# Five buffers for the values on their way out, a later fetch of the queries for the row maxima, and a later first subtraction of LayerNorm, in a gated attention and MLP block on one core

## The chip, the cores and the metric

The kernel runs on 1 core of one Trainium2 chip, as one launch. The metric is device microseconds of that launch; smaller is better. Times of whole runs are medians over a few runs; a profile is one further execution, taken with the hardware profiler. TensorE is PE in the rows (its weight loads are PEld), VectorE is DVE, ScalarE is ACT, GpSimd is POOL, SyncE is SP.

## The reference

One token block of 2048 rows and 448 features goes through two branches and a gate. Branch A is attention with 16 heads of 28 features, branch B a LayerNorm with a two-layer MLP of 1792 hidden features; a sigmoid of one dot product per row weighs them.

```python
def _A_ref(x, wqkv, wo):
    B, S, D = x.shape                      # 1, 2048, 448
    H = 16
    Dh = D // H
    qkv = (lambda x, *d: x.transpose(*d))((x @ wqkv).reshape(B, S, 3, H, Dh), 2, 0, 3, 1, 4)
    q, k, v = qkv[0], qkv[1], qkv[2]
    scores = jnp.einsum("bhqd,bhkd->bhqk", q, k) * (Dh ** -0.5)
    p = _softmax(scores, axis=-1)
    o = jnp.einsum("bhqk,bhkd->bhqd", p, v)
    return (lambda x, *d: x.transpose(*d))(o, 0, 2, 1, 3).reshape(B, S, D) @ wo

def _B_ref(x, w1, b1, w2, b2):
    y = _layernorm(x, axis=-1)
    h = _gelu(jnp.einsum("bsd,df->bsf", y, w1) + b1)
    return jnp.einsum("bsf,fd->bsd", h, w2) + b2

x = A_x
g = _sigmoid((x * gate_w).sum(-1, keepdims=True))
return g * _A_ref(x, A_wqkv, A_wo) + (1 - g) * _B_ref(x, B_w1, B_b1, B_w2, B_b2)
```

All arrays are float32. The kernel keeps that precision by splitting an operand into a rounded high part and a low rest and by adding three products (high by high, high by low, low by high).

## The kernel before

The program has two long parts, and both are ordered by hand: what PE does next is written out by Python code at build time.

**The strips** (class `Strips`, L404 to L538, up to about 455 us of the profile). PE is used as four strips of 32 rows. A tile of 128x512 (or 128x448) results lies in one PSUM bank; each strip adds its quarter of the contraction to it in a *visit* of 10 to 42 matmuls of 32 rows. Two strips don't visit a tile at the same time, and it is done when all four have. There are four kinds of tiles: `QK` (queries and keys, 28 of them), `Val` (the values with the gate's dot product as one more column, 16), `Up` (first MLP layer, 14 for each of four chunks of 512 tokens) and `Down` (second layer, 4 for each chunk). Six PSUM banks are for tiles, two (6 and 7) for row maxima.

**Row maxima.** The softmax needs a maximum for each query row before its exponentials are formed. It takes 1024 matmuls (L212: 28 rows of queries `qd` by 512 keys of `kd`), each followed by a `reduce_max` on DVE (L214). They are slipped between the visits whenever a planned bank and planned DVE time are free (`rowmax`, L497); what is left over at the end of the strips is slipped into the attention turns. They run in 16 problems `n` (4 groups of heads by 4 chunks of queries), problem `n` in buffer `qd[n % 2]`. When strip `j` has done its 16 matmuls of problem `n`, its quarter of the buffer is fetched anew for problem `n + 2` (`load_q`, L196, on SP's queue); after the last problem of a group its keys are fetched too (`load_k`, L180).

**The planner's clock.** The class simulates time: each matmul has a cost, each engine a time at which it comes free, and work of other engines is put on a list by `st.at(time, function)` and emitted when the planned time gets there. Only the order in which the instructions are emitted remains in the program; at run time each engine goes through its own list in order and waits on semaphores. A planned time that moves therefore moves instructions on every engine, and what PE does in the gaps changes with it.

**Handoffs.** When one strip ends its visit, the next strip may take the same bank only after it. This is signalled through SP: an increment of a semaphore, which waits for the last matmul of the visit, stands in SP's list, and the first matmul of the next visit waits for it. SP has the same list for its DMA issues, so an issue that waits, or that takes long, holds up the handoffs behind it.

```python
    sig = nc.sync.sem_inc(hand, 1)                                   # end of a visit, on SP (L529)
    tc.add_manual_dep(sig.ins, mm.ins.name, handoff, reason="handoff")
    ...
    if m == 0 and x.sig:                                             # start of the next one, on PE (L487)
        nc.tensor.wait_ge(hand, x.sig)
```

**Values on their way out.** When a `Val` tile is done, ACT copies it from PSUM to one of the buffers `vt` (L324) and a gate column to `zall` (L325), and then issues the store `vs<-vt` (L328) on its own queue. Tile `i` uses buffer `i % 3`. A copy waits until the store that used this buffer before has landed.

**LayerNorm.** For each chunk `c`, `want_ln` fetches the rows of mean and reciprocal deviation, spread over all partitions (`lnr`, L160, on POOL's queue), and four slices of x (`raw`, L571 on POOL's queue or, late, L569 on SP's). Each slice is then subtracted (L683 on DVE for chunks 0 and 1, L679 on POOL for 2 and 3), multiplied (L688 on POOL) and split into `yh` (L704, ACT) and `yl` (L705, POOL), which the `Up` tiles need. The same four slots `raw` also carry the weights w2 before that (w2's low parts are formed at L153 on POOL and DVE).

**The turns** (from about 455 us). Attention goes in turns of 5 or 6 units; a unit is 128 keys by 512 queries of one head, three score matmuls (L1152). After each half turn ACT forms exponentials of three or two banks at once (L1156), and PE multiplies them by the values (L1164). While row maxima are owed, a turn may have 5 units with three row-maximum matmuls, or 6 units with two; the planner takes as few turns of 5 as the owed number allows:

```python
size = min(left, 5 if owed and owed > 2 * ((left - 116) // 6) else 6)
```

Of the kernel before, what the change touches and what calls it, by code (L numbers as in the profile page):

```python
# [7 lines left out]
F32 = mybir.dt.float32  # L8
# [7 lines left out]
P = 128  # L16
S = 2048
D = 448
H = 16
# [16 lines left out]
def kernel(ctx: ExitStack, tc: tile.TileContext, xt, wqk, wv, wo, xk, w1, b1, w2, b2,  # L36
# [37 lines left out]
    bk = banks.tile([P, 8, CH], F32, name="bk")  # L74
# [3 lines left out]
    px = p0.enter_context(tc.tile_pool(name="px", bufs=1))  # L78
# [42 lines left out]
    mr = px.tile([P, 2, NT], F32, name="mr")  # L121
    mrt = px.tile([P, 2 * NT], F32, name="mrt")
    std = px.tile([P, NT], F32, name="std")
    vt = [px.tile([P, H, 32], F32, name=f"vt{i}") for i in range(3)]

    bxr = [px.tile([P, 2, D], F32, name=f"bxr{i}") for i in range(2)]

# [29 lines left out]
    def ln_rows_load(c):  # L157
        cs = slice(c * CH, (c + 1) * CH)
        lnr[c] = my.tile([P, 2, CH], F32, name="lnr")
        nc.gpsimd.dma_start(lnr[c], lns.rearrange("(n t) i -> n (t i)", n=2)[:, cs].partition_broadcast(P))  # L160

    class RowMax:
# [64 lines left out]
        def close(self, n):  # L227
            mf, mt = self.mf[n % 2], self.mt[n % 2]
            nc.vector.reduce_max(mf[:, 0:16], self.mx[n % 2].rearrange("p j i k -> p (j i) k"), axis=AX)
            nc.vector.transpose(mt, mf)  # L230
# [6 lines left out]
    rowmax = RowMax()  # L237
# [63 lines left out]
    class Val(Piece):  # L301
# [18 lines left out]
            return ops  # L320

        def close(self, st, now):
            v, ps, tt = vt[self.i % 3], bk[:, self.bank], self.i
            nc.scalar.activation(v[:, :, 0:DH], ps[:, :D].rearrange("p (h d) -> p h d", d=DH), AF.Copy)  # L324
            nc.scalar.activation(zall[:, tt:tt + 1], ps[:, D:D + 1], AF.Copy)  # L325
            st.use("act", now + 0.2, 0.75)
            st.free[self.bank] = st.act + 0.1
            st.at(st.act + 0.3, lambda: nc.scalar.dma_start(vs[tt], v.rearrange("p (g j) d -> p g (j d)", g=NG)), act=0.35)  # L328
# [75 lines left out]
    class Strips:  # L404
# [92 lines left out]
        def rowmax(self, s, now):  # L497
            if now < self.hot[s] or not rowmax.ready(s):
                return False
            if rowmax.cnt[s] > 5 + min(rowmax.cnt):  # L500
                return False
            b = min(self.rm, key=lambda b: self.rm[b])
            if self.rm[b] > now:
                return False
            ends = rowmax.one(s, bk[:, b])
            self.t[s] = now + 0.232
            self.use("dve", now + 0.45, RM)
            self.rm[b] = self.dve + 0.1
            for kind, n, j in ends:
                if kind == "q":  # L510
                    self.at(now + 1.5, lambda n=n, j=j: rowmax.load_q(n, j))
                elif kind == "k":
                    def load(n=n, j=j):
                        rowmax.load_k(n, j)
                        self.hot[j] = self.get(self.clock + 0.6, 224) + 1.0

                    self.at(now + 1.5, load)
                    self.hot[j] = 1e9
                else:
                    self.at(now + 0.5, lambda n=n: rowmax.close(n), dve=0.45)  # L520
                    self.at(now + 3.0, lambda n=n: rowmax.store(n))
            return True
# [151 lines left out]
    def want_ln(st, c):  # L674
        cs = slice(c * CH, (c + 1) * CH)

        def use(t, r):
            if c > 1:
                nc.gpsimd.tensor_sub(r, r, lnr[c][:, 0])  # L679
                st.use("pool", st.clock, 1.35)  # L680
                scale(t, r)
                return
            nc.vector.tensor_sub(r, r, lnr[c][:, 0])  # L683
            st.use("dve", st.clock, 1.2)
            st.at(st.dve + 0.15, lambda: scale(t, r))

        def scale(t, r):
            nc.gpsimd.tensor_mul(r, r, lnr[c][:, 1])  # L688
            st.use("pool", st.clock, 1.35)
            st.lns.setdefault(c, []).append((t, r, st.pool + 0.2))  # L690
            if c in st.go:
                split_y(st, c)

        for t in range(4):
            st.feed.add(xt[t, :, cs], 256, lambda r, t=t: use(t, r), kept=True,
                        first=(lambda: ln_rows_load(c)) if t == 0 else None)
        st.feed.pump()

    def split_y(st, c):
        while st.lns.get(c):  # L700
            t, r, end = st.lns[c].pop(0)

            def go(t=t, r=r):
                two(st, lambda: nc.scalar.activation(yh[:, t], r, AF.Copy),  # L704
                    lambda: nc.gpsimd.tensor_sub(yl[:, t], r, yh[:, t].bitcast(F32)), "pool", 1.35,  # L705
                    lambda end: then(r, end))

            def then(slot, end):
                st.feed.back(slot, end)
                st.yn[c] = st.yn.get(c, 0) + 1  # L710
                if st.yn[c] == 4:
                    st.yready[c] = end
                    if 0 < c < NC - 1:
                        st.at(end + 0.5, lambda: want_ln(st, c + 1))

            st.at(max(end, st.clock + 0.3), go)
# [173 lines left out]
    for i, key in enumerate(load):  # L890
        r = slots[i % 8]
# [361 lines left out]
```

## Time and profile before

| | us |
|---|---|
| median of 3 runs | 1094.56 |
| lowest and highest of them | 1093.5 and 1097.05 |
| the profiled execution | 1093.69 |
| its span, from the first to the last instruction | 1091.9 |
| PE busy within the span | 1074.4 (98%) |
| DVE, ACT, POOL busy | 740.4, 634.0, 368.7 |

The mean granted clock of TensorE is 0.996 of full speed. A "busy" PE is not PE at its peak: matmuls of the four strips overlap, and a matmul that waits a little behind others isn't seen as idle time. The chain of waits follows the work that ended last back from the end of the program and says, step by step, what released it. In a row of the timeline the bracket at the end tells how long the engine had been idle before it and who ended that. In a row of a window table the columns are the stretch, then for PE, PEld, DVE, ACT and POOL the busy time with the number of instructions, the granted clock, the busy share of the DMA engines and their rate in GB/s.

### The profile page before, as it was taken

Reading aid. Unit: us, or ns where it says so; the run is one execution under the profiler, and the core shown is the slowest. Engines: PE = TensorE matmul, PEld = TensorE weight load, DVE = VectorE, ACT = ScalarE, POOL = GpSimd, SP = SyncE. Lnnn points to the kernel's source line nnn. Section 1 sums busy time; section 2 is a strip of 40 time slices with the busy share of each in tenths; the row PEclk is TensorE's granted clock in tenths of the full one; section 3 lists DMA queues with packets and bytes.
Section 4 is the critical chain, followed back from the end, with each engine's and each line's share of the span. In section 5 each row is a group of like instructions: output and inputs, shape, how many; then the busy total and the mean of one; then the engine's idle time right before and its main releaser. Section 6 shows DMA issues by size and latency. Waiting matters only on the chain.

```text
span 1091.9 us, 30966 instructions
## 1 busy us (share of the span) xinstructions
PE 1074.4 (98%) x13394; PEld 728.4 (67%) x13394; DVE 740.4 (68%) x1186; ACT 634.0 (58%) x660; POOL 368.7 (34%) x384
## 2 busy tenths in 40 slices
PE   9999999999999999999999999999999999999998
PEld 7999998999899899844444444444444444454655
DVE  4899898898999999866776665667676544311102
ACT  5343363033043132287788788788787888857572
POOL 4565587336234037341001101310110313445431
PEclk9999999999999999999999999999999999999999
DMA  7696433212100104320000001300000201011111
GB/s 248 201 293 196 153 110 93 78 43 71 45 2 11 45 3 126 93 74 16 29 6 23 23 21 48 88 28 8 21 25 19 80 21 55 20 57 38 61 53 60
DMA packets 47785, 73.20 MB, mean 67 GB/s; under 512 B 13840, under 2 KB 28816, under 8 KB 46848
## 3 DMA queue, kind: packets, MB, share of 16 engines
q1 hardware_dynamic: 33888, 39.11, 11.8%
q0 software_dynamic: 5120, 16.89, 5.3%
q10 hardware_dynamic: 8640, 15.21, 3.9%
q8 instruction: 105, 1.72, 0.6%
q14 instruction: 32, 0.26, 0.1%
HBM read 51.75 MB, written 19.31 MB: 65 GB/s over the span
## 4 chain that ended last, share of the span: by engine, by line
PE 95%; ACT 1%; DMA 1%; DVE 1%; issue 1%; SPq 0%; DVEq 0%; ACTq 0%
PE bk L488 34%; PE bk L1164 22%; PE bk L1152 19%; PE bk L212 15%; PE bk L1001 1%; PE bk L1002 1%; PE bk L1003 1%; ACT p L1156 1%; PE bk L917 1%; DMA vs<-vt 1%; DMA gbs<-gb 1%; PE bk L902 0%; DVE ob L1023 0%; PE bk L945 0%; DVE acc L1008 0%
## 5 line engine op out<-in xcount | busy, mean ns | idle before, releaser
L214 DVE TENSOR_REDUCE mx<-bk 128x1 f32<-128x512 f32 x1024 | 674.2, 688 | 219.5 <-PE bk L212 188.4
L1156 ACT ACTIVATE p<-bk 128x1536 f32<-128x1536 f32 (+1 forms) x387 | 481.8, 1298 | 135.4 <-PE bk L1152 129.4
L212 PE MATMUL bk<-kd,qd 28*128 28x512 f32 x1024 | 449.2, 441 | 2.8 <-DVE acc L1008 1.7
L212 PEld LDWEIGHTS bk<-kd,qd 28*128 28x128 f32 x1024 | 186.4, 182 | 186.6 <-DVE mx L214 117.2
L488 PE MATMUL bk<-yh,w1f 32*128 32x512 f32 x1568 | 188.6, 393 | 2.5 <-ACT gb L398 2.5
L488 PE MATMUL bk<-yl,w1f 32*128 32x512 f32 x784 | 164.2, 393 | 0.0
L488 PEld LDWEIGHTS bk<-yh,w1f 32*128 32x128 f32 x1568 | 151.1, 183 | 5.7 <-ACT gb L398 3.7
L488 PE MATMUL bk<-w2h,hh 32*128 32x448 f32 x896 | 140.6, 368 | 2.2 <-SPq L529 2.2
L488 PE MATMUL bk<-w2l,hh 32*128 32x448 f32 x896 | 140.0, 366 | 0.0
L1164 PE MATMUL bk<-p,va 128*32 128x512 f32 (+1 forms) x1080 | 130.6, 579 | 0.0
L1164 PE MATMUL bk<-p,vb 128*32 128x512 f32 (+1 forms) x1192 | 129.4, 540 | 0.0
L363 POOL TENSOR_TENSOR hl<-h,hh 128x512 fp32r<-128x512 f32 x56 | 72.3, 1301 | 140.5 <-ACT hh L356 79.3
L837 POOL CAST yh<-yl 128x512 fp32r<-128x512 f32 x16 | 9.8, 614 | 285.7 <-PE bk L212 89.7
L1152 PE MATMUL bk<-yh,ka 29*128 29x512 f32 x512 | 104.3, 481 | 0.6 <-ACT p L1156 0.6
L488 PEld LDWEIGHTS bk<-w2h,hh 32*128 32x128 f32 x896 | 102.2, 185 | 3.3 <-SPq L529 2.6
L488 PEld LDWEIGHTS bk<-yl,w1f 32*128 32x128 f32 x784 | 103.3, 184 | 0.3
L488 PEld LDWEIGHTS bk<-w2l,hh 32*128 32x128 f32 x896 | 102.3, 185 | 0.1
L1152 PE MATMUL bk<-yh,kb 29*128 29x512 f32 x512 | 96.8, 478 | 0.7 <-ACT p L1156 0.5
L398 ACT ACTIVATE gb<-bk 128x448 f32<-128x448 f32 x14 | 7.6, 545 | 140.1 <-PE bk L488 98.8
L488 PE MATMUL bk<-w2h,hl 32*128 32x448 f32 x896 | 88.0, 362 | 0.0
L1152 PE MATMUL bk<-yh,la 28*128 28x512 f32 x512 | 86.3, 392 | 0.0
L1152 PE MATMUL bk<-yl,ka 28*128 28x512 f32 x512 | 84.7, 410 | 0.0
(141 smaller groups left out, 1603.5 us busy)
## 6 DMA issues: line engine op xcount, KB each, us to landing
qk<-qo ACTq DMA_DIRECT2D x28, 256.0 KB
raw<-in_xt SPq DMA_DIRECT2D x17, 256.0 KB
vs<-vt ACTq DMA_DIRECT2D x16, 256.0 KB
rc<-rls SPq DMA_DIRECT2D x60, 64.0 KB
bxr<-in_xk POOLq DMA_DIRECT2D x8, 448.0 KB, 6.1
acc<-gbs SPq DMA_DIRECT2D x16, 224.0 KB
out_y<-acc SPq DMA_DIRECT2D x16, 224.0 KB
qd<-qk SPq DMA_DIRECT2D x60, 56.0 KB
```

Of the source, the lines that this page charges most:

```text
L212: nc.tensor.matmul(ps, self.qd[n % 2][r, i * P:(i + 1) * P], self.kd[r, k * 512:(k + 1) * 512], start=True, stop=True)
L214: nc.vector.reduce_max(self.mx[n % 2][:, j, i, k:k + 1], ps, axis=AX)
L363: nc.gpsimd.tensor_sub(hl[f], h, hh[f].bitcast(F32))
L488: mm = nc.tensor.matmul(bk[:, x.bank, :n], a, b, start=x.first, stop=(len(x.rem) == 1 and m == len(ops) - 1), skip_group_check=True)
L837: nc.gpsimd.tensor_copy(h, l.bitcast(F32))
L917: nc.tensor.matmul(bk[:, b], w, v, start=(i == 0), stop=(i == len(ops) - 1), skip_group_check=True)
L1001: nc.tensor.matmul(po, h, woh[:, g], start=(g == 0), stop=False, skip_group_check=True)
L1002: nc.tensor.matmul(po, h, wol[:, g], start=False, stop=False, skip_group_check=True)
L1003: nc.tensor.matmul(po, l, woh[:, g], start=False, stop=(g == NG - 1), skip_group_check=True)
L1152: nc.tensor.matmul(bk[:, turn_bank(i)], w[r, ks], q[r], start=(p == 0), stop=(p == 2), skip_group_check=True)
L1156: nc.scalar.activation(t[:, :count], bk[:, b:b + count], AF.Exp, scale=SCALE)
L1164: nc.tensor.matmul(bk[32 * j:32 * j + 32, 7, sl], vg[n // NC][:, k, 32 * j:32 * j + 32], prob[4 * b + j][:, sl], start=(k == 0), stop=(k = ...
```

## The change

It does three things. `vt` has five buffers instead of three, and tile `i` uses buffer `i % 5`; two more pairs of small `memset` on POOL prepare them at the start. The fetch `load_q` is put on the planner's list 6.0 planned microseconds after the matmul that frees the buffer instead of 1.5 (in the strips; in the turns it stays one turn later). The first subtraction of chunk 0 is put on the list 1.5 planned microseconds after its slice has landed by the plan, instead of at once; chunk 1 stays on DVE as it was, chunks 2 and 3 on POOL.

```diff
-    vt = [px.tile([P, H, 32], F32, name=f"vt{i}") for i in range(3)]
+    vt = [px.tile([P, H, 32], F32, name=f"vt{i}") for i in range(5)]
...
-            v, ps, tt = vt[self.i % 3], bk[:, self.bank], self.i
+            v, ps, tt = vt[self.i % 5], bk[:, self.bank], self.i
...
                 if kind == "q":
-                    self.at(now + 1.5, lambda n=n, j=j: rowmax.load_q(n, j))
+                    self.at(now + 6.0, lambda n=n, j=j: rowmax.load_q(n, j))
...
-        def use(t, r):
+        def use(t, r, late=False):
             if c > 1:
                 nc.gpsimd.tensor_sub(r, r, lnr[c][:, 0])
                 st.use("pool", st.clock, 1.35)
                 scale(t, r)
+                return
+            if c == 0 and not late:
+                st.at(st.clock + 1.5, lambda: use(t, r, True))
                 return
             nc.vector.tensor_sub(r, r, lnr[c][:, 0])
             st.use("dve", st.clock, 1.2)
```

Since the order is planned, the change moves instructions on all engines from the middle of the `Val` tiles on. The 12 lines of the diff leave the work as it is, but of the 1024 row maxima 578 instead of 566 now stand before the first turn, and the turns have become 122 of 5 units and 69 of 6, where there were 136 of 5, 57 of 6 and a last one of 2; ACT issues 382 exponentials instead of 387.

Three places show what moved. The first is ACT in the middle of the `Val` tiles. `vt0_144` and so on are the buffers; L324 is the copy into one, L325 the gate column, L328 the store. Before:

```order
L328 DMA vs_88<-vt0_144 128x512
L328 DMA vs_88<-vt1_145 128x512
L324 ACTIVATE vt0_144<-bk_115 128x16x28
L325 ACTIVATE zall_68<-bk_115 128x1
L324 ACTIVATE vt2_146<-bk_115 128x16x28
```

and with the change:

```order
L328 DMA vs_88<-vt3_147 128x512
L328 DMA vs_88<-vt4_148 128x512
L324 ACTIVATE vt1_145<-bk_115 128x16x28
L325 ACTIVATE zall_68<-bk_115 128x1
L324 ACTIVATE vt0_144<-bk_115 128x16x28
```

Before, the copy of the third row goes into the buffer whose store is issued two rows above it; with the change it goes into one whose store was issued a pair of stores earlier.

The second is SP's list in the middle of the strips, where the slices of x for chunk 1 and then chunk 2 are fetched (L569 `raw<-in_xt`) and queries for the row maxima (L196 `qd<-qk`); the handoff increments stand between these rows and are not listed. Before:

```order
L569 DMA raw_132<-in_xt 128x512
L196 DMA qd_150<-qk 28x512
L569 DMA raw_133<-in_xt 128x512
L569 DMA raw_130<-in_xt 128x512
L569 DMA raw_131<-in_xt 128x512
L569 DMA raw_132<-in_xt 128x512
L196 DMA qd_150<-qk 28x512 x3
```

and with the change:

```order
L569 DMA raw_132<-in_xt 128x512
L569 DMA raw_133<-in_xt 128x512
L569 DMA raw_130<-in_xt 128x512
L569 DMA raw_131<-in_xt 128x512
L569 DMA raw_132<-in_xt 128x512
L196 DMA qd_152<-qk 28x512
L233 DMA ms_74<-mt_158 4x32x32
L196 DMA qd_152<-qk 28x512 x3
```

The fetch of queries that stood ahead of the four slices of chunk 2, and the one right behind them, have moved behind. Read in the built program, with the handoffs and counting PE's matmuls from the start: before, the last handoff ahead of the four slices reports matmul 2865, and the next increments behind them and the fetch are waited for by PE at matmuls 2896, 2915 and, much later, 3069. With the change the last one ahead reports matmul 2849, and the next ones are waited for at 2941, 2936 and 3026.

The third is DVE around the subtractions of chunk 0 (L683, which is L686 in the changed file; L214 are the reductions of the row maxima). Before:

```order
L214 TENSOR_REDUCE mx_153<-bk 128x1 x17
L683 TENSOR_TENSOR raw_131<-raw_131,lnr 128x512
L214 TENSOR_REDUCE mx_153<-bk 128x1 x2
L683 TENSOR_TENSOR raw_132<-raw_132,lnr 128x512
L683 TENSOR_TENSOR raw_133<-raw_133,lnr 128x512
L214 TENSOR_REDUCE mx_153<-bk 128x1
L683 TENSOR_TENSOR raw_130<-raw_130,lnr 128x512
```

and with the change:

```order
L214 TENSOR_REDUCE mx_155<-bk 128x1 x19
L686 TENSOR_TENSOR raw_131<-raw_131,lnr 128x512
L214 TENSOR_REDUCE mx_155<-bk 128x1 x2
L686 TENSOR_TENSOR raw_132<-raw_132,lnr 128x512
L686 TENSOR_TENSOR raw_133<-raw_133,lnr 128x512
L214 TENSOR_REDUCE mx_155<-bk 128x1 x2
L686 TENSOR_TENSOR raw_130<-raw_130,lnr 128x512
```

Each subtraction stands two or three reductions later.

## The prediction, made before the result was known

> **What bounds the kernel now.** The page comes first, for how full PE is and which chain ended last.
>
> ```profile
> span 1091.9 us, 30966 instructions
> PE 1074.4 (98%) x13394; PEld 728.4 (67%) x13394; DVE 740.4 (68%) x1186; ACT 634.0 (58%) x660; POOL 368.7 (34%) x384
> PE 95%; ACT 1%; DMA 1%; DVE 1%; issue 1%; SPq 0%; DVEq 0%; ACTq 0%
> ```
>
> PE is 95% of the chain, so a gain is either time in which PE stands or runs slowly, or fewer PE microseconds for the same work. I looked for the first kind in the list of waits of PE, and in window tables for the two parts.
>
> ```profile
> PE bk L488 <- ACT gb L398: 2.5, 2, 1.4
> PE bk L488 <- SPq L529: 2.2, 1, 2.2
> PE bk L488 <- ACT zall L325: 1.9, 1, 1.9
> 16.00:455.00 439.00, 432.37 (x7332) 412.46 (x7332) 400.55 (x643) 139.99 (x250) 215.99 (x225) 0.99 0.31 97
> 200.00:300.00 100.00, 98.93 (x1729) 94.01 (x1725) 93.86 (x148) 24.60 (x40) 39.01 (x32) 1.00 0.16 51
>   PEld bk L212: 0.6, 3
> ```
>
> The strips hold four visible stalls of PE, 6.6 us in all; outside them a strip matmul costs 98.93/1729 = 0.057 us. DVE has 38 us of idle time there. The last row, from the view of the row-maximum tile in the strips, says that PE's weight loads waited for DVE three times, 0.6 us in all. So the strips are bound by PE's order. Two of the four stalls are where the change works.
>
> **Stall A: the values on their way out.** ACT's timeline, then PE's, then DVE's, then the windows.
>
> ```profile
> 97.89 0.33 ACTq L328 DMA_DIRECT2D vs<-vt  x1
> 101.34 0.55 ACT L324 ACTIVATE vt<-bk 128x448 f32<-128x448 f32 x1 [0.70 <-PE bk L488]
> 101.41 0.33 ACTq L328 DMA_DIRECT2D vs<-vt  x1
> 108.77 0.54 ACT L324 ACTIVATE vt<-bk 128x448 f32<-128x448 f32 x1 [6.83 <-DMA vs<-vt]
> 114.05 0.55 ACT L324 ACTIVATE vt<-bk 128x448 f32<-128x448 f32 x1 [4.17 <-PE bk L488]
> 107.17 0.36 PE L488 MATMUL bk<-wvs,xl 32*128 32x450 f32 x1
> 109.43 0.47 PE L488 MATMUL bk<-wvs,xh 32*128 32x450 f32 x1 [1.90 <-ACT zall L325]
> 98.67 9.19 DVE L214 TENSOR_REDUCE mx<-bk 128x1 f32<-128x512 f32 x14 [0.37 <-PE bk L212]
> 109.98 0.69 DVE L214 TENSOR_REDUCE mx<-bk 128x1 f32<-128x512 f32 x1 [2.13 <-PE bk L212]
> 112.65 0.69 DVE L214 TENSOR_REDUCE mx<-bk 128x1 f32<-128x512 f32 x1 [0.49 <-PE bk L212]
> 107.00:108.00 1.00, 0.53 (x11) 0.16 (x3) 0.85 (x2) 0.00 (x0) 0.00 (x0) 1.00 0.99 381
> 109.00:110.00 1.00, 0.57 (x8) 0.56 (x12) 0.01 (x1) 0.88 (x4) 0.00 (x0) 0.89 0.34 131
> 110.00:111.00 1.00, 1.00 (x16) 1.00 (x16) 1.00 (x2) 0.00 (x0) 0.00 (x0) 0.50 0.83 315
> 112.00:113.00 1.00, 1.00 (x16) 1.00 (x12) 0.51 (x2) 0.00 (x0) 0.63 (x1) 0.50 0.00 0
> ```
>
> The copy at 108.77 goes into the buffer whose store was issued at 101.41, and that store lay for 7.3 us in the burst of LayerNorm's fetches. PE needs the bank: nothing starts from 107.17 to 109.43, 2.2 us beyond the usual gap. Then the clock is at 0.50 for three windows and 0.89 and 0.90 beside them, another 1.7 us. From both sides: 2.2 us if the slow stretch hides under other waits, 3.9 if it all counts. DVE, which reduces without a break before and after, loses 2.13 + 0.49 and a few tenths between, 2.8. I take 3.0, near DVE's number.
>
> With five buffers that copy waits for the store issued at 97.89. Before, the copy at 101.34 waits for that same store, and it waited for PE alone: the store had landed by then. What is late next is the third pair of copies, 114.05 here; less the 3.9 us it comes at about 110.1, and the one of its two stores that matters is the one of 101.41 again, landed at 108.7. That leaves 1.4 us, so no wait.
>
> **The subtraction.** DVE would reach the old place of the first subtraction 0.65 us after its last reduction (107.86), at 108.5, while the fetches still run (0.99 busy at 107, idle at 112). Two reductions later (17.58 us for 27 of them, below) it is 109.8. The slices behind it come at 110.5 or more. I take zero for the wait; the bounds are -0.7 (the place now reached was needed) and +1.5 (rival 3). The four extra `memset` are 0.5 us on POOL before 2 us and lie under the first loads.
>
> **Stall B: handoffs behind DMA issues.** SP, POOL, PE, DVE and the windows.
>
> ```profile
> 187.96 2.58 SPq L569 DMA_DIRECT2D raw<-in_xt  x4
> 190.65 8.93 SPq L196 DMA_DIRECT2D qd<-qk  x3
> 184.89 2.55 POOL L705 TENSOR_TENSOR yl<-raw,yh 128x512 fp32r<-128x512 f32 x2
> 189.16 0.36 PE L488 MATMUL bk<-w2h,hh 32*128 32x448 f32 x1
> 191.74 0.73 PE L488 MATMUL bk<-w2h,hh 32*128 32x448 f32 x1 [2.22 <-SPq L529]
> 192.61 0.69 DVE L214 TENSOR_REDUCE mx<-bk 128x1 f32<-128x512 f32 x1 [2.78 <-PE bk L212]
> 192.00:193.00 1.00, 1.00 (x12) 0.96 (x16) 0.39 (x1) 0.00 (x0) 0.00 (x0) 0.50 0.95 227
> 194.00:195.00 1.00, 1.00 (x18) 1.00 (x14) 0.69 (x1) 0.00 (x0) 0.24 (x1) 0.50 0.81 299
> 120.24 17.58 DVE L214 TENSOR_REDUCE mx<-bk 128x1 f32<-128x512 f32 x27 [1.17 <-PE bk L488]
> ```
>
> The handoff that PE waits for at 191.74 stands behind four slice fetches (0.65 us each) and one fetch of queries. The handoff ahead of them reports matmul 2865, and PE wants the one behind at 2896: 31 matmuls, 1.8 us, for 2.9 us of issuing. PE stands 2.5 us, and three windows at half clock add 1.5. DVE's idle time says the same: 2.78, and 1.2 in the two gaps that follow. So B costs 4.0.
>
> With the change SP begins on the four fetches after matmul 2849 and the next handoff is wanted at 2936: 87 matmuls, 5.0 us, for 2.6 us of issuing. The last fetch also waits for the last `yl` of chunk 1, which ended at 187.44; its subtractions stand 18 matmuls later, so about 188.4. Then SP is free at 189.5, and 2936 comes at 189.2 + 40 x 0.057 = 191.5. I take the full 4.0; the lower bound is 0, if POOL falls back by more than 2 us.
>
> The later fetch of queries has no price of its own: its buffer is next read 16 matmuls per strip, some 42 us of reductions, later. What it does is leave SP's list shorter at such places.
>
> **The turns.** The first exponential, and the groups of those started in 460 to 855.2 us (turns of 5), 868.1 to 932.4 (turns of 6 with two row maxima) and 935.6 to 960.9 (turns of 6 without):
>
> ```profile
> 456.88 2.37 ACT L1156 ACTIVATE p<-bk 128x1536 f32<-128x1536 f32 x2 [0.53 <-PE bk L1152]
> L1156 ACT ACTIVATE p<-bk 128x1536 f32<-128x1536 f32 (+1 forms) x268 | 317.2, 1235 | 78.5 <-PE bk L1152 72.5 <-PE bk L212 5.9
> L1156 ACT ACTIVATE p<-bk 128x1536 f32<-128x1536 f32 x40 | 55.8, 1449 | 8.7 <-PE bk L1152 8.6
> L1156 ACT ACTIVATE p<-bk 128x1536 f32<-128x1536 f32 x16 | 22.3, 1449 | 3.2 <-PE bk L1152 3.2
> ```
>
> Two per turn: 395.2/134 = 2.95, 64.3/20 = 3.21 and 25.3/8 = 3.16 us. The change has 15 turns of 5 fewer (its last turn apart), 16.5 more of 6 with two row maxima, 4.5 fewer of 6 without, and a last turn of 5 units for one of 2: -44.2 + 53.0 - 14.2 + 3 x 0.59 = -3.6. The 12 row maxima that moved cost 12 x 0.057 = 0.7 in the strips. Net -2.9. Bounds: -3.6, if the strips have idle strips for them, and +3.5, if each costs DVE's 17.58/27 = 0.65 there.
>
> **What it gives back**, with a wait of SP that a rival needs:
>
> ```profile
> SPq L569 <- POOL w2l L153: 2.5, 1, 2.5
> 379.91 0.54 ACT L398 ACTIVATE gb<-bk 128x448 f32<-128x448 f32 x1 [3.00 <-DMA gbs<-gb]
> 453.80 0.54 ACT L398 ACTIVATE gb<-bk 128x448 f32<-128x448 f32 x1 [0.46 <-PE bk L488]
> ```
>
> The copies out of `Down` tiles have two buffers and wait for their stores as before; their order shifts by some matmuls. After chunk 0 the last copy now comes sooner behind the others (+0.8), after chunk 2 they are farther apart (-0.6). At the end of the strips the first turn now needs the last of four such copies, which go 1.0 us apart, where it needed the third: +0.6. Together +0.8, between 0 and 2.
>
> **Sum** against the profiled execution's own time: 1093.69 - 3.0 - 4.0 - 2.9 + 0.8 = 1084.6. The median shown is 0.9 above that execution, so 1085.5 for the median.
>
> **The rivals.** A measurement of this kernel tells 0.3%, 3.3 us, from no change: 1091.3 to 1097.8.
>
> 1. The forecast, 1085.5. Its own range is 1083 (A 3.9, B 4.2, turns 3.6) to 1090 (A 2.2, B 2.5, turns 1.5). Chance 0.50.
> 2. Handoffs are held up at another place: B's cost stays, 1089.5. For it: the plan does not know SP's issue times, and all fetches of w2 and of x still stand in SP's list. Against it: I found no handoff left with so little room behind several issues. 0.22.
> 3. The stall of the values only changes its owner: two stores (512 KB) now join the burst while LayerNorm's slices still come, at the 381 GB/s of the row at 107 us they delay them by 1.4 us, DVE waits at a subtraction with row maxima behind it, and PE's two banks for them fill. A gives 1.0 instead of 3.0: 1087.5. 0.10. [...]
> 4. The 12 row maxima cost DVE's time in the strips: 1085.5 + 7.1 = 1092.6. Against it: the 38 us of idle DVE. 0.08.
> 5. The other side: SP's fetches of w2 stand between handoffs and wait for slots that POOL frees (one such wait, of 2.5 us, before). If the moved order lets SP wait there three times, at B's 4.2 us each with the slow clock, the time is 1085.5 + 12.6 = 1098.1; it decides from the second, which takes it to no change. 0.07.
> 6. The change doesn't do what it says: A and B stay, only the turns gain: 1092.5. 0.03.
>
> Faster: 0.48 of the first, 0.20 of the second, 0.09 of the third, 0.77. Within 0.3%: 0.16, of cases 4 and 6 and the slow ends of 1 to 3. Slower: 0.07. The range reaches from 1082.5, the fast end of 1, over 2 and 3 to 1093, behind 4 and 6.
>
> **What would show it.** Right: no wait of ACT L324 for `vs<-vt` near 108 us and no clock of 0.50 at 110; no wait of PE for SP near 190; first exponential 6 us or more earlier than 456.88; 191 turns with the same prices, and an end 3 us closer behind it. Wrong: a wait of DVE at its subtraction for `lnr` or `raw`; a wait of PE for SP in 140 to 165 us; or strips that end no earlier although both stalls are gone, which would say that DVE or the plan's own gaps set their pace.

## The result and the profile after

| | before | changed |
|---|---|---|
| median of 6 runs, us | 1094.51 (1091.62 to 1097.88) | 1086.76 (1083.9 to 1087.95) |
| ratio of the changed kernel to before | | 0.9924, 95% interval 0.9901 to 0.9947 |
| the profiled execution, us | 1093.69 | 1083.9 |
| its span, us | 1091.9 | 1082.1 |

The changed kernel is faster by 7.75 us in the medians (8.3 by the ratio); the forecast was 1085.5, in a range of 1082.5 to 1093. The profiled executions differ by 9.8 us, where the forecast's sum had 9.1. The profile after, first its page:

```profile
span 1082.1 us, 31042 instructions
...
PE 1068.2 (99%) x13434; PEld 724.8 (67%) x13434; DVE 739.9 (68%) x1186; ACT 633.9 (59%) x655; POOL 368.2 (34%) x388
```

Then two rows of its list of PE's waits (us in total, times, the longest), the only one for `L488` and that for the row maxima's keys:

```profile
PE bk L212 <- DMA kd<-qk: 1.0, 1, 1.0
...
PE bk L488 <- ACT gb L398: 0.3, 1, 0.3
```

And the window of the strips:

```profile
16.00:455.00 439.00, 438.64 (x7391) 417.27 (x7394) 408.73 (x658) 144.85 (x254) 217.53 (x229) 1.00 0.33 102
```

Of PE's 6.6 us of visible stalls in the strips 0.36 is left, the clock is at 1.00, and neither SP nor `zall` is among what PE waited for. (The wait for `kd` lies in the turns.) The two places of the prediction come next: ACT's timeline around the values,

```profile
106.48 0.55 ACT L324 ACTIVATE vt<-bk 128x448 f32<-128x448 f32 x1 [4.31 <-PE bk L488]
...
110.51 0.55 ACT L324 ACTIVATE vt<-bk 128x448 f32<-128x448 f32 x1 [2.92 <-PE bk L488]
```

DVE's,

```profile
98.90 11.11 DVE L214 TENSOR_REDUCE mx<-bk 128x1 f32<-128x512 f32 x17 [0.36 <-PE bk L212]
109.92 0.68 DVE L686 TENSOR_TENSOR raw<-raw,lnr 128x512 f32<-128x512 f32 x1
```

SP's around the fetches of chunk 2 (the first row joins the issues of chunk 1 and chunk 2),

```profile
166.53 20.43 SPq L569 DMA_DIRECT2D raw<-in_xt  x8
190.39 0.34 SPq L196 DMA_DIRECT2D qd<-qk  x1
```

and a window at each place:

```profile
105.00:115.00 10.00, 10.00 (x191) 9.75 (x190) 9.91 (x16) 2.85 (x9) 3.56 (x3) 1.00 0.69 259
185.00:195.00 10.00, 10.00 (x184) 9.70 (x182) 9.85 (x17) 0.00 (x0) 3.58 (x4) 1.00 0.65 179
```

The copies into `vt` now wait for PE alone, DVE goes from reductions into the subtraction at 109.92 without a wait, and PE is busy all through both windows. Last, the first exponential in ACT's timeline,

```profile
450.70 1.45 ACT L1159 ACTIVATE p<-bk 128x1536 f32<-128x1536 f32 x1 [0.65 <-PE bk L1155]
```

and two groups of exponentials, those of 453.8 to 816.6 us (turns of 5) and of 840.3 to 937.6 us (turns of 6 with two row maxima):

```profile
L1159 ACT ACTIVATE p<-bk 128x1536 f32<-128x1536 f32 x245 | 290.8, 1240 | 72.9 <-PE bk L1155 72.9
L1159 ACT ACTIVATE p<-bk 128x1536 f32<-128x1536 f32 x61 | 85.1, 1449 | 11.7 <-PE bk L1155 11.7
```

The strips end 6.2 us earlier (456.88 to 450.70), and what lies behind the first exponential is 3.6 us shorter (1091.9 - 456.88 = 635.0, 1082.1 - 450.70 = 631.4). A turn costs what it did: 362.8/122.5 = 2.96 and 97.3/30.5 = 3.19 us.

One execution is not the median, though. In a second profile of the same program, taken beside the experiments, the span is 1085.4 us and the first exponential comes at 454.37. A row of its list of PE's waits, and ACT's timeline:

```profile
PE bk L488 <- ACT gb L398: 2.0, 3, 1.4
```

```profile
377.23 0.54 ACT L398 ACTIVATE gb<-bk 128x448 f32<-128x448 f32 x1 [3.21 <-DMA gbs<-gb]
...
454.37 2.37 ACT L1159 ACTIVATE p<-bk 128x1536 f32<-128x1536 f32 x2 [0.70 <-PE bk L1155]
```

There the fourth copy out of the `Down` tiles of chunk 2 waits for its store, as it did before the change; in the first profile it waited for PE alone. The standstills of both profiles and of all experiments are set side by side behind the experiments.

### The profile page after: what moved, and what is told of

Read it like the earlier page. It is cut to its first block, busy times and chain, and to the rows that moved or that the text cites. A ratio compares the mean times of both kernels' runs of the same rounds, so it can differ in the third digit from the quotient of the medians.

```text
span 1082.1 us, 31042 instructions
## 1 busy us (share of the span) xinstructions
PE 1068.2 (99%) x13434; PEld 724.8 (67%) x13434; DVE 739.9 (68%) x1186; ACT 633.9 (59%) x655; POOL 368.2 (34%) x388
## 3 DMA queue, kind: packets, MB, share of 16 engines
q8 instruction: 105, 1.72, 0.7%
## 4 chain that ended last, share of the span: by engine, by line
PE 96%; ACT 1%; DMA 1%; DVE 1%; issue 0%; SPq 0%; DVEq 0%; ACTq 0%
PE bk L488 35%; PE bk L1167 22%; PE bk L1155 19%; PE bk L212 15%; PE bk L1004 1%; ACT p L1159 1%; PE bk L1005 1%; PE bk L1006 1%; PE bk L920 1%; DMA first<-in_xt 1%; DMA kd<-qk 0%; DVE acc L1011 0%; PE bk L948 0%; DMA gbs<-gb 0%; DVE ob L1026 0%
## 5 line engine op out<-in xcount | busy, mean ns | idle before, releaser
L214 DVE TENSOR_REDUCE mx<-bk 128x1 f32<-128x512 f32 x1024 | 673.7, 688 | 218.5 <-PE bk L212 178.7
L1159 ACT ACTIVATE p<-bk 128x1536 f32<-128x1536 f32 x382 | 481.1, 1313 | 128.8 <-PE bk L1155 127.2
L488 PE MATMUL bk<-yh,w1f 32*128 32x512 f32 x1568 | 192.3, 393 | 0.4 <-ACT gb L398 0.3
L488 PE MATMUL bk<-yl,w1f 32*128 32x512 f32 x784 | 167.1, 391 | 0.0
L488 PEld LDWEIGHTS bk<-yh,w1f 32*128 32x128 f32 x1568 | 154.4, 183 | 2.4 <-ACT gb L398 1.1
L488 PE MATMUL bk<-w2h,hh 32*128 32x448 f32 x896 | 145.2, 366 | 0.0
L488 PE MATMUL bk<-w2l,hh 32*128 32x448 f32 x896 | 144.2, 364 | 0.0
L488 PEld LDWEIGHTS bk<-yl,w1f 32*128 32x128 f32 x784 | 105.7, 183 | 0.2
L488 PEld LDWEIGHTS bk<-w2h,hh 32*128 32x128 f32 x896 | 102.7, 183 | 0.5
L488 PEld LDWEIGHTS bk<-w2l,hh 32*128 32x128 f32 x896 | 102.5, 183 | 0.3
L1155 PE MATMUL bk<-yh,ka 29*128 29x512 f32 x512 | 101.5, 482 | 0.6 <-ACT p L1159 0.6
L488 PE MATMUL bk<-w2h,hl 32*128 32x448 f32 x896 | 93.2, 363 | 0.0
L1155 PE MATMUL bk<-yh,la 28*128 28x512 f32 x512 | 83.7, 393 | 0.0
```

Source lines behind the costliest of these rows:

```text
L214: nc.vector.reduce_max(self.mx[n % 2][:, j, i, k:k + 1], ps, axis=AX)
L488: mm = nc.tensor.matmul(bk[:, x.bank, :n], a, b, start=x.first, stop=(len(x.rem) == 1 and m == len(ops) - 1), skip_group_check=True)
L1155: nc.tensor.matmul(bk[:, turn_bank(i)], w[r, ks], q[r], start=(p == 0), stop=(p == 2), skip_group_check=True)
L1159: nc.scalar.activation(t[:, :count], bk[:, b:b + count], AF.Exp, scale=SCALE)
```

## The experiments

The three edits are independent enough to be taken alone and left out. The order of PE's instructions depends on the later subtraction only: with it, it is that of the changed kernel, without it, that of before, whatever the other two edits are. A last kind of kernel takes a suspected wait away by itself. The ratios are to runs of the kernel before on the same chip; 0.001 is 1.1 us.

### Each edit alone, and stall B alone

**Only the five buffers** (the first two lines of the diff).

> Only the five buffers; everything else as before, and PE's order is that of before. Theory (stall A is the wait of the copy for its store): no wait of ACT L324 near 108 us, no clock of 0.50 at 110, the stall near 189 us stays, first exponential near 453.9 instead of 456.88, median 3.0 lower: 1091.5. Rival (the stall changes its owner): DVE waits at its first subtraction for lnr or raw, gain about 1.0: 1093.5.

Ratio 0.9959, interval 0.9940 to 0.9978: 4.5 us faster, between 2.4 and 6.6. The timelines of ACT and DVE, then PE's waits:

```profile
106.92 0.54 ACT L324 ACTIVATE vt<-bk 128x448 f32<-128x448 f32 x1 [4.31 <-PE bk L488]
```

```profile
109.08 0.68 DVE L683 TENSOR_TENSOR raw<-raw,lnr 128x512 f32<-128x512 f32 x1
```

```profile
PE bk L488 <- SPq L529: 2.1, 1, 2.1
```

The wait for the store is gone, stall B stays, and the subtraction at its old place doesn't wait either. (A standstill of 0.57 us at 110 us comes before another matmul than stall A did, and the profile shows no releaser for it.) So the buffers cure stall A alone, and the rival of a new owner falls. The size is the 3.0 of the theory or more.

**Only the slices of chunk 2 apart.** SP's list is the only thing that changes:

```diff
-                if st.late:
+                if st.late and st.apart is not None:
+                    st.at(st.clock + 1.5 * st.apart, lambda t=t, src=src: nc.sync.dma_start(t, src))
+                    st.apart += 1
+                elif st.late:
                     nc.sync.dma_start(t, src)
...
+        st.apart = 0 if c == 2 else None
         st.feed.pump()
+        st.apart = None
```

> Before, with only the four slice fetches of chunk 2 put on the planner's list 0, 1.5, 3.0 and 4.5 planned us after each other's start instead of all at once, so that handoffs get between them in SP's list; PE's order is that of before. Theory (stall B is the handoff behind five issues, and costs 2.5 us of standing and 1.5 us of half clock): no wait of PE for SP near 189 us and no window at clock 0.50 there, median 4.0 lower: 1090.5. Rival 1: the half clock there has another cause and stays, gain 2.5: 1092. Rival 2: DVE's reductions set the pace and take the time back by the end of the chunk, gain under 1: 1094.

Ratio 0.9967, 0.9950 to 0.9984: 3.6 us faster, between 1.7 and 5.5. SP's timeline, and the window of 189 to 196 us, first of the kernel before and then of this one:

```profile
185.51 0.34 SPq L570 DMA_DIRECT2D raw<-in_xt  x1
185.90 0.41 SPq L196 DMA_DIRECT2D qd<-qk  x1
187.02 1.40 SPq L570 DMA_DIRECT2D raw<-in_xt  x2
...
189.56 1.13 SPq L570 DMA_DIRECT2D raw<-in_xt  x1
```

```profile
189.00:196.00 7.00, 4.78 (x61) 4.37 (x57) 2.95 (x6) 0.00 (x0) 1.24 (x1) 0.76 0.78 235
```

```profile
189.00:196.00 7.00, 7.00 (x141) 6.69 (x137) 6.74 (x13) 0.00 (x0) 3.96 (x4) 1.00 0.62 174
```

PE no longer stands, and 141 matmuls run in that window; in the profile of before it held 61, at a clock of 0.76. So stall B is the handoff behind the issues, and its price of 4.0 lies within the interval.

**Only the later subtraction.**

> Only the later first subtraction of chunk 0; three buffers, queries fetched after 1.5 us as before. PE's order is that of the changed kernel. Theory (this edit alone moves PE's order, and with it both cures stall B and brings the 12 row maxima forward): B 4.0 and turns 2.9 gained, 0.8 given back, stall A stays: median 1088.4, no wait of PE for SP near 189. Rival (the later query fetch is what cures B, and without it SP's five issues near 410 us hold up a handoff): only the turns gain, 1092.4, with a wait of PE for SP.

Far from the theory: 0.9984, 0.9967 to 1.0001, so 1.7 us faster instead of 6.1, and not told from no change. Its profile has no wait of PE for SP, so stall B is cured by this edit as expected, and the rival falls too. But stall A has grown, and the new order costs time elsewhere (below). ACT's timeline and PE's waits:

```profile
111.92 0.54 ACT L324 ACTIVATE vt<-bk 128x448 f32<-128x448 f32 x1 [9.14 <-DMA vs<-vt]
```

```profile
PE bk L488 <- ACT zall L325: 4.2, 1, 4.2
```

**Only the later fetch of queries.**

> Only the queries for the row maxima fetched 6.0 instead of 1.5 planned us later; PE's order is that of before. Theory (the fetch has no price of its own): it takes one issue of 0.65 us out of the list ahead of the handoff at 191.74, PE waits for SP there 1.6 instead of 2.2 us: median 1093.8. Rival (the distance of this fetch is the cure of stall B): no wait of PE for SP near 189, 1090.5. If a row maximum waits for its queries later, slower than 1094.5.

Again not as expected: 0.9969, 0.9950 to 0.9989, 3.4 us faster instead of 0.7. The wait for SP is 1.6 us, as the theory had it, so the rival's mechanism isn't there. What differs is behind the wait. This kernel's windows at stall B, and at the `Down` copies of chunk 2:

```profile
187.00:188.00 1.00, 0.94 (x17) 0.54 (x9) 1.00 (x2) 0.00 (x0) 0.00 (x0) 1.00 0.55 145
188.00:189.00 1.00, 0.00 (x0) 0.00 (x0) 0.26 (x1) 0.00 (x0) 0.00 (x0) 1.00 0.92 229
189.00:190.00 1.00, 0.43 (x8) 0.42 (x12) 0.00 (x0) 0.00 (x0) 0.00 (x0) 1.00 1.10 301
190.00:191.00 1.00, 1.00 (x26) 1.00 (x22) 0.78 (x2) 0.00 (x0) 0.00 (x0) 1.00 0.93 207
...
376.00:377.00 1.00, 0.00 (x0) 0.00 (x0) 0.00 (x0) 0.07 (x1) 0.00 (x0) 1.00 0.06 22
377.00:378.00 1.00, 0.48 (x8) 0.44 (x12) 0.00 (x0) 0.54 (x2) 0.00 (x0) 1.00 0.00 0
378.00:379.00 1.00, 1.00 (x24) 0.80 (x20) 0.88 (x2) 0.97 (x2) 0.00 (x0) 0.78 0.61 228
379.00:380.00 1.00, 1.00 (x16) 0.85 (x12) 0.51 (x1) 0.28 (x1) 0.59 (x1) 0.50 0.06 10
```

A standstill of 1.6 us at stall B keeps the full clock; one of 1.8 us at 376 is followed by half clock. With one issue less in SP's list, stall B in this profile costs 1.6 us, where it cost 2.2 and 1.7 of half clock before: 2.3 us less, within the interval of 1.2 to 5.5. This second part is read from one profile of each.

### Each edit left out

These four ran on one chip. **The changed kernel again**, **without the buffers**, **without the later fetch** and **without the later subtraction**, each the changed kernel with that edit undone.

> The changed kernel itself, beside the next three on the same chip. It was 0.9924 of before; on the chip of the single edits (before 1092.9) that is 1084.6. No idle stretch of PE of more than 0.5 us in the strips, no half clock.

> The changed kernel with three buffers again. Theory (the single edits overlap: in the new order the wait of the copy for its store is 2 us or more, and a standstill of PE of about 1.7 us or more is followed by 1.7 us of half clock): a standstill of PE near 108 us, 3.6 to 7.6 us slower than the changed kernel, 1090 on a chip where before is 1092.9. Rival (the price of the wait is that of the old order, without half clock): 1.5 us, 1086.

> The changed kernel with the queries fetched after 1.5 planned us again. Theory (in the new order no handoff stands behind SP's fetches anyway; the later fetch is worth its 3.4 us only where stall B is): within 0.7 us of the changed kernel, 1085, no wait of PE for SP, at most a short one near 410 us where five issues stand in 3.7 us. Rival (the later fetch is worth 3 us in any order): 1088.

> The changed kernel with the first subtraction at its old place: five buffers and the later fetch in the order of before. Theory (A 3.9 gone, stall B 1.6 us without half clock, turns as before): 1092.9 - 3.9 - 2.2 = 1086.8, 2.2 above the changed kernel, a wait of PE for SP near 187 us. Rival (the single gains 4.5 and 3.4 simply add): 1085.0, no difference to the changed kernel that can be told.

| | ratio | interval | median, us |
|---|---|---|---|
| changed kernel again | 0.9918 | 0.9904 to 0.9933 | 1086.14 |
| without the buffers | 0.9943 | 0.9925 to 0.9961 | 1088.29 |
| without the later fetch | 0.9922 | 0.9906 to 0.9937 | 1086.15 |
| without the later subtraction | 0.9940 | 0.9925 to 0.9955 | 1088.83 |

The buffers are worth 2.7 us here, between theory and rival: the standstill near 108 us came back with 1.45 us and no half clock. The changed kernel's own expectation failed in two points, standstills of 0.7 us near 195 and 1.4 us near 376. The later fetch is worth nothing once no handoff stands behind SP's fetches, as expected, and the later subtraction about what was expected, 2.4 us. (The intervals of the kernels without the buffers and without the later subtraction overlap a little with that of the changed kernel.) With the old order PE waits 1.6 us for SP again. The single gains, 4.5, 3.4 and 1.7, aren't properties of the edits: the later fetch and the later subtraction both take from stall B, and what one takes the other can't.

### Two kernels a second time

**Only the later subtraction**, and **the changed kernel without the buffers**.

> The kernel with only the later subtraction a second time. Theory (how long the store lies in the burst differs from execution to execution of one program): the standstill near 108 us is 1.4 to 2.2 us this time, not 4.2, and the ratio comes nearer to that of the kernel with the later fetch beside it, 0.995 to 0.997. Rival (this edit alone makes the store land 3 us later): a standstill of 4 us with 3.4 us of half clock again, ratio 0.998.

> The kernel with the later fetch and the later subtraction, without the buffers, a second time, since it came out 4 us below the kernel with the later subtraction alone in ratio (0.9943 against 0.9984, twice). Theory (the later fetch has no price where no handoff stands behind SP, and the two were compared against different samples of before): 0.996 to 0.998 this time, about 1090, with a standstill of 1.4 us or more near 108 us. Rival (the later fetch shortens the wait of the copy for its store also with three buffers): 0.994 again, 1088, and a standstill of 1.5 us or less.

The first was 0.9984 again, 0.9964 to 1.0004, but with a standstill of 1.84 us and no half clock in its profile:

```profile
108.31 0.54 ACT L324 ACTIVATE vt<-bk 128x448 f32<-128x448 f32 x1 [6.79 <-DMA vs<-vt]
```

So the length of this wait differs between executions of one program, as the theory had it, though the ratio didn't come nearer. The second was 0.9962, 0.9942 to 0.9982. The two kernels differ in the later fetch alone; by the second pair (0.9984 and 0.9962) the intervals overlap, by the first pair (0.9984 and 0.9943) they don't. Whether the later fetch also helps with three buffers in the new order stays open. The buffers' worth in that order, from both runs each: 0.9953 against 0.9921, 3.5 us.

### The standstills taken away in both orders

**The changed kernel with the `Down` copies in four buffers**: the last two of each chunk use the buffers `h`, as those of the last chunk did already.

```diff
-            if self.c == NC - 1 and self.i > 1:
+            if self.i > 1:
                 gb = mhp[0].tile([P, CH], F32, name="h", bufs=2)[:, :D]
```

**The old order with its four standstills taken away**: this edit, five buffers, the later fetch, the slices apart, and the first subtraction at its old place.

> The changed kernel, with the last two copies out of the Down tiles of every chunk (not only of the last) put into the two buffers h, which the Up tiles use between. PE's order is that of the changed kernel. Theory (the copies' waits for their stores are all that still stands in the strips, 0.4 to 2.3 us): no idle stretch of PE near 214, 294 and 376 us, median 1.5 lower, ratio to before 0.990. Rival (the next Up tile's GELU then waits for the store out of h): a wait of PE or ACT near 218, 299 or 381, no gain, 0.992.

> The order of PE of the kernel before, with its four standstills taken away: five buffers, the later fetch, the slices of chunk 2 fetched apart, and the Down copies as in the run beside it. Theory (before is slow by its standstills and the half clock behind them, 6.6 and 3.4 us): ratio 0.991, first exponential near 447, 1084.5 where before is 1094.5; the new order then owes its gain to the standstills, and its 12 row maxima less in the turns are paid back in the strips. Rival (the new order is better by itself, by the 2.9 of the turns): 2.9 us slower than the changed kernel with the same copies, 0.993 against 0.990.

Ratios 0.9917 (0.9898 to 0.9935) and 0.9923 (0.9904 to 0.9942); medians 1084.07 and 1084.43 us, beside 1092.86 of before. The copies' waits at 214, 294 and 376 are gone from the first, but against the changed kernel (0.9924 and 0.9918) no gain can be told. The rival had that number, but its wait isn't there: the GELUs near 218, 295 and 377 us wait for PE, not for a store. What matters is the second: the old order reaches the same time once its standstills are taken away (the two medians, of six runs each on one chip, are 0.4 us apart). The new order isn't better by itself, and the rival of 2.9 us falls. The first exponential in ACT's timeline, of the old order and then of the new, both cleared:

```profile
447.59 2.37 ACT L1162 ACTIVATE p<-bk 128x1536 f32<-128x1536 f32 x2 [0.50 <-PE bk L1158]
```

```profile
451.28 2.37 ACT L1159 ACTIVATE p<-bk 128x1536 f32<-128x1536 f32 x2 [0.70 <-PE bk L1155]
```

### The standstills of all profiles

From windows of 1 us between 93 us and the end of the strips: idle time of PE at the four places, and behind a plus what the windows' clock lacks of full speed. "Rest" is the first exponential less all of these and a few smaller ones: the strips without standstills. "Behind" is the span less the first exponential. The 0.6 to 0.9 us near 108 in the kernels with five buffers come before another matmul than stall A's, and the 0.2 to 0.7 of the new order in the column of SP lie near 196 us; for neither does the profile show a releaser.

| profile | values, near 108 | SP, near 188 | Down, near 293 | Down, near 376 | first exponential | rest | behind |
|---|---|---|---|---|---|---|---|
| **old order:** before | 1.9 + 1.7 | 2.2 + 1.7 | 1.1 | 1.4 | 456.9 | 446.9 | 635.0 |
| only the buffers | 0.6 | 2.1 + 1.7 | 1.7 | 1.0 | 454.6 | 447.4 | 633.4 |
| only slices apart | 1.5 | 0 | 1.6 + 1.7 | 1.1 | 452.0 | 446.1 | 635.0 |
| only the later fetch | 1.4 | 1.6 | 1.3 | 1.8 + 1.7 | 455.2 | 447.2 | 633.4 |
| without the later subtraction | 0.7 | 1.6 | 1.7 | 1.3 | 452.8 | 447.5 | 634.7 |
| old order cleared | 0.7 | 0 | 0.2 | 0.5 | 447.6 | 446.1 | 634.7 |
| **new order:** changed | 0 | 0 | 0.3 | 0 | 450.7 | 450.4 | 631.4 |
| changed, again | 0 | 0.7 | 0.4 | 1.4 | 454.4 | 451.7 | 631.0 |
| without the buffers | 1.5 | 0 | 0.7 | 1.3 | 454.9 | 451.3 | 631.4 |
| without them, again | 1.7 | 0 | 0.5 | 1.4 | 455.1 | 451.4 | 631.7 |
| without the later fetch | 0.7 | 0.2 | 0.5 | 1.2 | 455.5 | 452.7 | 631.2 |
| only the later subtraction | 4.2 + 3.4 | 0 | 0.2 | 0 | 458.9 | 450.7 | 632.5 |
| only that, again | 1.8 | 0.4 | 0.1 | 1.2 | 455.1 | 450.9 | 632.4 |
| new order, four Down buffers | 0.9 | 0.7 | 0 | 0 | 451.3 | 449.6 | 631.4 |

The rest is 446.1 to 447.5 in the old order and 449.6 to 452.7 in the new, whatever stood still. In the mean the new order is 4.2 us longer in the strips (446.9 and 451.1) and 2.8 us shorter behind them (634.4 and 631.6). Profiles of one order differ by up to 3.1 us in the rest and 1.7 us behind, so these means are worth more than a single pair of profiles.

Where it is longer shows in two windows over the MLP of chunk 0, here of the old order cleared:

```profile
142.00:173.00 31.00, 31.00 (x521) 29.74 (x519) 26.60 (x40) 20.18 (x36) 25.53 (x21) 1.00 0.45 127
173.00:215.00 42.00, 42.00 (x760) 40.10 (x757) 41.40 (x63) 6.03 (x10) 21.61 (x18) 1.00 0.21 68
```

and of the new one with four Down buffers:

```profile
142.00:173.00 31.00, 31.00 (x487) 29.46 (x484) 27.97 (x42) 21.59 (x38) 24.99 (x21) 1.00 0.40 111
173.00:215.00 42.00, 41.30 (x741) 39.86 (x734) 38.58 (x62) 4.71 (x8) 22.54 (x18) 1.00 0.24 78
```

1281 matmuls and 1228: 53 fewer, at 0.057 us 3.0 us, of which 0.7 is the standstill near 195. PE counts as busy, but its matmuls stand farther apart. The first of the two windows reads alike in other profiles: 514 matmuls in the old order with the slices apart, 492 in the changed kernel, 489 with only the later subtraction (its second run). DVE isn't fuller there (68.0 and 66.6 us), so it isn't the moved row maxima that fill it.

The programs themselves show what thins PE out. They say to which strip each matmul belongs, and in the strips the profile's records can be laid beside them one by one. Mostly PE's list goes round the four strips, so that a matmul stands four places behind the last one of its own strip. A matmul that stands only two or three places behind gained nothing by it: in the profile of the old order cleared it starts 0.20 us (median) after a matmul of 448 columns and 0.23 us after one of 512, as those four places behind do. So a strip that is listed again early lets PE finish fewer matmuls in the same time, while PE still counts as busy. Of matmuls 2500 to 3000 of the list (163 to 194 us), 77 stand less than four places behind in the old order and 148 in the new, and these 500 matmuls take 27.7 us in the old order cleared and 29.7 in the new one with four `Down` buffers: about half of the 4.2. An estimate for the whole list up to the first score matmul, with each strip doing one matmul after the other at the medians above, 0.204 us (448 columns) or 0.232 (512), and no wait of any kind, is 432.5 us for the old order and 436.7 for the new: the 4.2 us, the 12 row maxima included. This is read from the lists and the traces; no run evened out the strips of the new order.

## Why the prediction came out right, and where it was wrong

**Stall A, 3.0.** Right in its mechanism, its place (110.51 for the third pair of copies, where 110.1 was worked out) and its size: 4.5 us alone, in an interval of 2.4 to 6.6, and 3.5 in the new order. But the standstill it was sized on isn't a constant. In the seven profiles with three buffers it is 1.4 to 1.9 us in six and 4.2 in one, with half clock behind it in two. That 3.0 lies between its bounds of 2.2 and 3.9 was a choice, and the runs don't tell it from either.

**The subtraction, zero.** Right. DVE reached the new place at 109.92 (109.8 was worked out) and didn't wait; nor did it at the old place with five buffers, 109.08.

**Stall B, 4.0.** Right: 3.6 us (1.7 to 5.5) with the slices apart and all else as before. Of the three edits the later subtraction is the one that removes it altogether, by the moved order.

**The later fetch, no own price.** Wrong for the old order, right for the new one with five buffers. The prediction saw that it leaves SP's list shorter, and did not price that at stall B: one issue less, which took 0.98 us in the profile of before (190.65 us; the expectation had 0.65), and in the profile also no half clock.

**The turns, 2.9.** The step that failed. The gain behind the first exponential came as worked out, with the same prices per turn (2.96 for 2.95): 3.6 us in the first profile, 2.8 in the mean of all. Its price in the strips was put at 12 x 0.057 = 0.7, and the new order as a whole costs 4.2 there. The bounds for it, -3.6 to +3.5, held the net of +1.4, but the value taken was near the wrong end. The prediction priced the moved row maxima alone, as if the rest of the order stayed as dense as it was; the loss lies where the order of everything else moved, and by the lists of the two programs it is the new order's less even use of the four strips. Rival 4, that DVE pays 0.65 for each, has the size partly and the mechanism not, as DVE isn't fuller in that stretch.

**What it gives back, 0.8.** Wrong in sign. The waits of PE for the `Down` copies fell from 2.5 us to 0.3 in the first profile and to 2.0 in the second. After chunk 0, put at 0.8, a wait of 0.2 us came in the second profile and none in the first. The end of the strips, put at 0.6, shows 0.1: from the first of the last four copies to the first exponential it is 4.08 us before (452.80 to 456.88) and 4.22 with the change (446.48 to 450.70).

**The sum** therefore met the result in part by luck, by terms that offset each other. By the table, the first profile has 10.0 us of standstills and half clock before and 0.3 after, 9.7 us less; the order's rest is 3.5 longer there and the part behind 3.6 shorter; 9.8 in all, as measured. In the second profile 2.7 us of standstills are left, so 7.3 less; the rest is 4.8 longer and the part behind 4.0 shorter, 6.5 in all. Either way the gain is made of standstills only. Of the rivals, handoffs held up elsewhere (2), a new owner of the values' stall (3), SP's w2 fetches (5) and a change without effect (6) didn't come: no profile in the new order has a wait of PE that the list puts down to SP, though a short standstill near 196 us, 0.2 to 0.7 us in four of its eight profiles, has no releaser that the profile shows.

## What to carry to other kernels

Where an order is planned by hand or by a planner, separate a change's order from the waits it happens to remove: take the same waits away in the old order, and compare the two cleared of them. Price a moved piece not by its own instructions alone but by how dense the new order is around it, stretch by stretch, in instructions per microsecond; where PE works in strips, count in the list how often a strip comes again before the other three have had their turn. And look at more than one profile before sizing a standstill that a DMA ends.

## What the runs showed of the hardware

**The half clock came in one amount.** Wherever a standstill of PE in the strips was followed by half clock, the windows lack 1.69 to 1.71 us of full speed, that is 3.4 us at 0.50, whether the standstill was 1.56, 1.84, 1.90, 2.13 or 2.22 us; with the one of 4.20 it was twice that, 3.41, part of it while PE still stood. Standstills of 1.55 us and less never had it; of those from 1.56 to 1.84 two had it (1.56 and 1.84) and six did not (1.59, 1.64, 1.66, 1.72 twice and another 1.84). What decides it between these, no run shows. In these profiles each standstill of 1.9 us or more lost at least 1.7 us more than itself, and those of 1.55 us and less only themselves.

**A store's landing is not a constant of the program.** The same kernel's copy waited 9.14 us for its store in one profile and 6.79 in another, and with the first, half clock followed: the spans are 1091.4 and 1087.5 us.

**Within a strip, matmuls started 0.20 or 0.23 us apart.** In the profile of the old order cleared the start of a matmul follows that of the last one in its strip by 0.20 us (median, 448 columns) or 0.23 us (512), whether it stands two, three or four places behind it in PE's list. Of matmuls 2500 to 3000, the list with 77 that stand less than four places behind took 27.7 us, the one with 148 took 29.7.
